# Turns of the first expert layer rounded by ScalarE's integer write, and q's second order of halves copied instead of transposed

## The chip, the cores and the metric

One NeuronCore of a Trainium2 chip runs the whole program. The metric is the device time of one execution in microseconds (us), as the median of several executions. Beside it stands one profiled execution with its trace. The engines are named as the profile names them: PE (TensorE, with PEld for its weight loads), DVE (VectorE), ACT (ScalarE), POOL (GpSimd) and SP (SyncE, whose queue "SPq" issues all DMAs here).

## What is computed

Attention over 4 batches and 8 heads (1152 keys of 64 elements, q averaged in pairs to 576 rows), and behind it two dense layers over the 2304 tokens. The first has `h*cos(h)` as its nonlinearity, the second `h*sigmoid(h)`.

```python
q_pool = q.reshape(B, H, S // 2, 2, D).mean(axis=3)
scores = scale * np.matmul(q_pool, k.transpose(0, 1, 3, 2))
attn = softmax(scores)                      # with 1e-09 in the denominator
x = heads_side_by_side(np.matmul(attn, v))  # 2304 x 512
h = x @ w_in;   x = (h * np.cos(h)) @ w_out         # 512 -> 2048 -> 512
h = x @ w_in2;  out = (h / (1 + np.exp(-h))) @ w_out2
```

## The kernel before

**Halves.** Every matmul input is kept as two fp16 numbers, a high half and the rest ("low" half), which takes two or three fp16 matmuls for one product.

**Attention.** Two heads make a pair; there are 16 pairs (4 per batch). A pair has 9 tiles of 128 query rows, 144 in all. For a tile, PE writes scores into two PSUM tiles `sp` (line 549), DVE scales them into `sc` and takes their minimum (line 568), ACT takes the exponential (line 576) and writes the high half `hl` (line 582), POOL writes the low half in three pieces (line 150, called from line 587), SP issues one DMA transpose of both halves, 18 blocks of 128x128 (line 589), and PE multiplies by v (lines 600, 604). Up to four tiles are in flight.

**Preparing a pair** (`pair_prep`, lines 473 to 532) runs during the tiles of the pair before: maxima on DVE (line 127), a scale, then the halves of q, k and v. For q the array `qn` holds the halves twice, once in the order high|low and once low|high, because keys come as high|low and both products are wanted: ACT writes the high half in two places (line 509), DVE the low half (line 510) and a second copy of it (line 513), and one DMA transpose of 18 blocks makes `qT` (line 515). `kn` is split by ACT and DVE (lines 466, 471) and transposed, 18 blocks (line 525).

**First layer.** It works on 9 blocks of 256 tokens. A unit is 12 matmuls: 16 units of the first product (`h`, line 685) and 16 of the second (`y`, line 740) in a block. From batch 1 on, two units are handed out for each attention tile; what remains comes behind attention, beside the preparation of the second layer's weights. Two units of the first product fill one PSUM tile; there are two of these. ACT copies it to `hk`, scaled so that 1 is a full turn (line 701). Four units make a group `hk` of 128x1024, 36 groups in all. Then `g_cos_begin` works out the distance to the nearest whole turn on DVE: line 713 adds 0.25 and a large number that rounds, line 714 subtracts the number and `hk`. ACT takes the sine (line 720), DVE multiplies (line 723) and writes the high half `gh` (line 728), POOL the low half `gl` (line 150). The array `tt` has two buffers; a block's result `y32` (line 749), on its way to DRAM, uses the same two.

**Second layer.** Behind that PE alternates between the second layer's two products.

**What sets the order.** Each engine runs its own list in order. The lists are made when the program is built, by a scheduler that works with priorities and its own time model. A change of one instruction can so move others.

Of the kernel before, what the change touches and what calls it, by code (L numbers as in the profile page):

```python
# [11 lines left out]
F32 = mybir.dt.float32  # L12
F16 = mybir.dt.float16
I32 = mybir.dt.int32
AF = mybir.ActivationFunctionType
ALU = mybir.AluOpType
# [2 lines left out]
DRAM = bass.MemoryType.DRAM  # L19

EXP_MASK = 0x7F800000
MAGIC = 12582912.0
TINY = 2.0**-50
W_MIN = float(np.array([0x38100000], np.uint32).view(np.float32)[0])
END = object()
P_CH, P_SC, P_EX, P_PV, P_MS, P_MU, P_W, P_PR, P_X = 0, 60, 0, -100, 200, 0, 0, 0, 0
PSH = 15.0
NB_N, NB_SC, NB_H, NB_T, NB_S = 2, 4, 4, 4, 5
LOW_HL, LOW_G, LOW_W = 3, 2, 2
X_LAG = 40  # L30
W1_BUFS, WT_BUFS = 3, 3
# [8 lines left out]
NB_HK, NB_TT, NB_G, SIN_N = 2, 2, 2, 2  # L40
# [9 lines left out]
def attention_moe_moe_kernel(ctx, tc, q, k, v, w_in1, w_out1, w_in2, w_out2, out):  # L50
# [3 lines left out]
    nc = tc.nc  # L54
    B, H, S, D = q.shape
# [4 lines left out]
    KC = S // 128  # L60
# [5 lines left out]
    const = ctx.enter_context(tc.tile_pool(name="const", bufs=1))  # L66
# [6 lines left out]
    mean = const.tile([128, 128], F32, name="mean")  # L73
    halfpi = const.tile([128, 1], F32, name="halfpi")
    floor3 = const.tile([128, 1], F32, name="floor3")

    def make_consts():
        nc.vector.memset(mean, 2.0**-7)
        nc.vector.memset(halfpi, math.pi / 2)
        nc.vector.memset(floor3, 2.0**-14 - 0.5)  # L80

    GW = 256

# [389 lines left out]
    def pair_prep(at, P):  # L473
        NQ = 2 * NT + 1
        qs = P.q[:, :, 0, :]
# [28 lines left out]
            split(vt[:, :, 0, 0:D], vt[:, :, 1, 0:D], P.v[i], s[:, 2:3], P.on_pool >= 2)  # L504


        qn = at.src.tile([128, 2, NQ, 2, D], F16, tag="kn", name="qn", bufs=NB_N)
        for e in range(2):
            nc.scalar.activation(out=qn[:, e, :, e, :], in_=qs, func=AF.Copy, scale=s[:, 0:1])
        nc.vector.scalar_tensor_tensor(  # L510
            out=qn[:, 0, :, 1, :], in0=qs, scalar=s[:, 0:1], in1=qn[:, 0, :, 0, :], op0=ALU.mult, op1=ALU.subtract
        )
        nc.vector.tensor_copy(qn[:, 1, :, 0, :], qn[:, 0, :, 1, :])
        qT = at.p.tile([128, 2, NQ, 128], F16, tag="qT", name="qT", bufs=2)
        nc.sync.dma_start_transpose(
            out=qT.rearrange("p e n k -> p (e n) k"), in_=qn.rearrange("p e n s d -> p (e n s d)")
        )
        P.qT = [qT[:, e] for e in range(2)]
        yield
        kn = at.src.tile([128, 2, KC, 2, D], F16, tag="kn", name="kn", bufs=NB_N)  # L520
        for i in range(2):
            split(kn[:, i, :, 0, :], kn[:, i, :, 1, :], P.k[i], s[:, 1:2], P.on_pool >= 1)
            yield
# [6 lines left out]
        for i in range(2):  # L530
            do_v(i)
            yield

    segs = [(o, min(512, S - o)) for o in range(0, S, 512)]

# [155 lines left out]
    def g1_evac(mp, w, blk, f, first):  # L691
        if f % 2 == 0:
            return
        g = f * w.npc // NF
        if first:
            if f % 4 == 1:
                blk.hk = mp.p.tile([128, 4, GW], F32, tag="hk", name="hk", bufs=NB_HK)
            o = blk.hk[:, (f % 4) - 1:(f % 4) + 1, :]
        else:
            o = blk.view(f - 1, 2)  # L700
        nc.scalar.activation(  # L701
            out=o, in_=blk.hp, func=AF.Copy if first else AF.Silu, scale=blk.c.a[:, g:g + 1]
        )

    def g_cos_begin(mp, blk):

        G = Block()
        G.hk, G.K = blk.hk, blk.c.k
        G.gh = mp.p.tile([128, 4, GW], F16, tag="gh", name="gh", bufs=NB_G)
        G.gl = mp.p.tile([128, 4, GW], F16, tag="gl", name="gl", bufs=NB_G)  # L710
        blk.g.append((G.gh, G.gl))
        G.t = t = mp.p.tile([128, 4, GW], F32, tag="tt", name="tt", bufs=NB_TT)
        nc.vector.tensor_scalar(out=t, in0=G.hk, scalar1=0.25, scalar2=MAGIC, op0=ALU.add, op1=ALU.add)
        nc.vector.scalar_tensor_tensor(out=t, in0=t, scalar=MAGIC, in1=G.hk, op0=ALU.subtract, op1=ALU.subtract)
        return G

    def g_cos_end(groups):
# [553 lines left out]
```

## Time and profile before

| | |
|---|---|
| median of 3 runs | 1358.67 us (1353.96 to 1359.51) |
| the profiled execution | 1361.32 us, span of the trace 1359.5 us |
| busy in the span | PE 1146.0 (84%), PEld 914.5 (67%), DVE 981.6 (72%), ACT 870.0 (64%), POOL 705.1 (52%) |
| DMA queue | 509,472 packets, 65.7% of 16 engines over the span |
| granted TensorE clock | 0.916 of full speed over the span |

The span has four stages, told apart by what PE does: attention alone (0 to about 240 us), attention with units of the first layer (240 to about 816), the rest of the first layer beside the weights of the second (816 to about 1059), and the second layer (1059 to the end). A busy share says how much of a stretch an engine worked; the waits say what ended the idle time before an instruction.

### The profile page before, as it was taken

What the parts mean: (1) busy time and instruction counts of PE and PEld (TensorE: products, weight loads), DVE (VectorE), ACT (ScalarE), POOL (GpSimd) and SP (SyncE); (2) the same over time, 40 slices, a digit from 0 to 9 for tenths busy, and PEclk for the clock granted to TensorE, in tenths of its full rate; (3) what the DMA queues carried; (4) which work ended last, traced back from release to release, by engine and by line L of the source; (5) the groups of instructions that cost most, each with busy time, mean ns of one, the idle gap of its engine ahead of it and who ended that gap; (6) DMA issues with size and microseconds to landing.
All of it is one profiled execution on the core that took longest, in us unless ns stands there. A gap on an engine that the chain in (4) does not pass through costs nothing. (4 is left out here: it accounts for less than half of the span.)

```text
span 1359.5 us, 26737 instructions
## 1 busy us (share of the span) xinstructions
PE 1146.0 (84%) x10668; PEld 914.5 (67%) x10668; DVE 981.6 (72%) x1927; ACT 870.0 (64%) x1061; POOL 705.1 (52%) x624
## 2 busy tenths in 40 slices
PE   1564565888988679998898999899999999999998
PEld 0333343666766456675676677788788888888887
DVE  6896978877877777795787795986757755444483
ACT  3896888778777777885788774634546633333352
POOL 1688686688668576875768673533667400000000
PEclk9677676989999888998999999999899999999999
DMA  9999999889799999998999975413344000000001
GB/s 270 210 229 219 224 242 208 152 159 175 139 191 186 195 201 202 191 162 161 164 181 190 197 174 100 128 60 75 82 97 106 32 30 27 9 16 17 17 32 32
DMA packets 509597, 186.29 MB, mean 137 GB/s; under 512 B 465952, under 2 KB 484384, under 8 KB 509472
## 3 DMA queue, kind: packets, MB, share of 16 engines
q1 hardware_dynamic: 509472, 184.59, 65.7%
q8 instruction: 83, 1.36, 0.4%
q14 instruction: 42, 0.34, 0.1%
HBM read 66.58 MB, written 9.44 MB: 56 GB/s over the span
## 5 line engine op out<-in xcount | busy, mean ns | idle before, releaser
L150 POOL TENSOR_TENSOR hl<-sc,hl 128x384 f16<-128x384 f32 x432 | 453.8, 1081 | 145.3 <-ACT hl L582 110.1
L568 DVE TENSOR_SCALAR_CACHE_REDUCE sc<-sp,psu 128x512 f32<-128x512 f32 (+1 forms) x288 | 229.7, 808 | 78.1 <-PE sp L549 66.9
L549 PE MATMUL sp<-kT,qT 128*128 128x512 f16 (+1 forms) x768 | 195.3, 373 | 83.5 <-DVE sc L568 58.7
L685 PEld LDWEIGHTS <-ih 128*128 128x128 f16 x2304 | 226.3, 100 | 45.7 <-issue 13.8
L600 PE MATMUL pv<-vt,hlT 128*128 128x130 f16 (+1 forms) x1440 | 194.6, 236 | 73.8 <-DMA hlT<-hl 68.2
L576 ACT ACTIVATE sc<-sc,nb 128x1152 f32<-128x1152 f32 x144 | 179.4, 1249 | 76.8 <-DVE nb L573 69.7
L600 PEld LDWEIGHTS <-hlT 128*128 128x128 f16 (+1 forms) x1440 | 144.6, 109 | 106.3 <-DMA hlT<-hl 80.9
L685 PE MATMUL h<-ys,ih 128*128 128x256 f16 x1152 | 195.6, 274 | 4.1 <-ACT gs L701 4.1
L685 PE MATMUL h<-xT,ih 128*128 128x256 f16 x1024 | 186.3, 277 | 5.1 <-ACT hk L701 2.1
L604 PE MATMUL pv<-vt,hlT 128*128 128x65 f16 (+1 forms) x1440 | 184.7, 206 | 0.0
L582 ACT ACTIVATE hl<-sc 128x1152 f16<-128x1152 f32 x144 | 165.2, 1154 | 26.2 <-DMA hlT<-hl 20.0
L549 PEld LDWEIGHTS <-qT 128*128 128x128 f16 x768 | 77.1, 109 | 150.9 <-issue 102.5
L740 PE MATMUL y<-gh,oh 128*128 128x256 f16 x576 | 162.8, 283 | 6.8 <-ACT y L749 6.8
L740 PE MATMUL y<-gl,oh 128*128 128x256 f16 x576 | 163.1, 283 | 1.9 <-POOL gl L150 1.9
L740 PE MATMUL y<-gh,ol 128*128 128x256 f16 x576 | 162.6, 282 | 0.0
L854 PEld LDWEIGHTS <-op 128*128 128x128 f16 x1512 | 147.9, 98 | 18.0 <-issue 0.6
L685 PE MATMUL h<-ys,il 128*128 128x256 f16 x576 | 157.7, 274 | 0.0
L604 PEld LDWEIGHTS <-hlT 128*128 128x128 f16 (+1 forms) x1440 | 141.2, 107 | 14.6 <-issue 7.1
L685 PE MATMUL h<-xT,il 128*128 128x256 f16 x512 | 141.8, 277 | 0.0
L150 POOL TENSOR_TENSOR gl<-tt,gh 128x512 f16<-128x512 f32 (+1 forms) x60 | 97.3, 1637 | 79.7 <-DVE gh L728 61.0
L740 PEld LDWEIGHTS <-oh 128*128 128x128 f16 x1152 | 115.4, 102 | 30.8 <-issue 10.3
L685 PEld LDWEIGHTS <-il 128*128 128x128 f16 x1152 | 114.2, 99 | 16.9 <-issue 0.4
(310 smaller groups left out, 1967.6 us busy)
## 6 DMA issues: line engine op xcount, KB each, us to landing
wst<-in_moe_w_in_dram SPq DMA_DIRECT2D x16, 1024.0 KB, 6.1
stk<-in_k_dram SPq DMA_DIRECT2D x32, 288.0 KB, 4.2
stv<-in_v_dram SPq DMA_DIRECT2D x32, 288.0 KB, 4.4
stq<-in_q_dram SPq DMA_DIRECT2D x32, 256.0 KB, 3.1
wst<-in_moe_w_out_dram SPq DMA_DIRECT2D x8, 1024.0 KB, 6.4
wst<-in_moe_w_out_dram SPq DMA_DIRECT2D x16, 512.0 KB, 6.0
ydr<-y SPq DMA_DIRECT2D x9, 512.0 KB, 3.3
y32b<-ydr SPq DMA_DIRECT2D x9, 512.0 KB, 3.3
```

What stands on the lines that cost most here:

```text
L150: last = nc.gpsimd.tensor_tensor(out=lo[:, o:o + w], in0=x[:, o:o + w], in1=hi[:, o:o + w], op=ALU.subtract)
L549: nc.tensor.matmul(sp[:, o - a:o - a + n], P.qT[e][:, t, :], kT[:, o:o + n], start=(e == 0), stop=(e == 1))
L568: nc.vector.tensor_scalar(out=T.sc[:, a:z], in0=sp, scalar1=T.P.su, scalar2=None, op0=ALU.mult, op1=ALU.min, accum_out=mx[:, x:x + 1],)
L576: nc.scalar.activation(out=T.sc, in_=T.sc, func=AF.Exp, scale=-1.0, bias=nb)
L582: nc.scalar.activation(out=hi, in_=T.sc, func=AF.Copy)
L600: nc.tensor.matmul(G.pv[r, T.gi], T.hlT[:, 0, c, r], P.vt[i][:, c], start=(c == 0), stop=(c == KC - 1), skip_group_check=True,)
L604: nc.tensor.matmul(G.pv[r, T.gi, 0], T.hlT[:, 1, c, r], P.vt[i][:, c, 0], start=False, stop=(c == KC - 1), skip_group_check=True,)
L685: nc.tensor.matmul(hp, wt[:, c, f * 128:(f + 1) * 128], xt(c), start=(i == 0), stop=(i == 3 * NC - 1), skip_group_check=True,)
L740: nc.tensor.matmul(blk.y[:, oc, :], wt[:, f, oc * 128:(oc + 1) * 128], gt[:, f % 4, :], start=(f == 0 and e == 0 and oc % 2 == 0), stop=(f ...
L854: nc.tensor.matmul(bank, t[:, e, c, :], wt[:, c, :], start=start, stop=True, skip_group_check=True)
```

## The change

Two edits.

1. *Turns.* The array `tt` is now taken together with `hk`, at the first of a group's two evictions. ACT reads each PSUM tile a second time and writes `hk + 0.25` into `tt` as a 32-bit integer, which rounds to a whole turn. On DVE the two instructions of lines 713 and 714 become one, integer minus `hk`.
2. *q.* `qn` holds the halves once. One ACT instruction writes the high half, one DVE instruction the low half, and the DMA transpose has 9 blocks where it had 18. The other order is made from the result: two ACT copies of 64 partitions x 1152 elements swap the upper and the lower 64 partitions. They stand at the end of the pair's preparation, with a step of their own. `qn` and `kn` have one buffer each, where they shared two.

```diff
-        qn = at.src.tile([128, 2, NQ, 2, D], F16, tag="kn", name="qn", bufs=NB_N)
-        for e in range(2):
-            nc.scalar.activation(out=qn[:, e, :, e, :], in_=qs, func=AF.Copy, scale=s[:, 0:1])
-        nc.vector.scalar_tensor_tensor(
-            out=qn[:, 0, :, 1, :], in0=qs, scalar=s[:, 0:1], in1=qn[:, 0, :, 0, :], op0=ALU.mult, op1=ALU.subtract
-        )
-        nc.vector.tensor_copy(qn[:, 1, :, 0, :], qn[:, 0, :, 1, :])
+        qn = at.src.tile([128, NQ, 2, D], F16, tag="qn", name="qn", bufs=1)
+        split(qn[:, :, 0, :], qn[:, :, 1, :], qs, s[:, 0:1], False)
         qT = at.p.tile([128, 2, NQ, 128], F16, tag="qT", name="qT", bufs=2)
-        nc.sync.dma_start_transpose(
-            out=qT.rearrange("p e n k -> p (e n) k"), in_=qn.rearrange("p e n s d -> p (e n s d)")
-        )
+        nc.sync.dma_start_transpose(out=qT[:, 0], in_=qn.rearrange("p n s d -> p (n s d)"))
...
+        for x, y in ((slice(0, 64), slice(64, 128)), (slice(64, 128), slice(0, 64))):
+            nc.scalar.activation(out=qT[x, 1], in_=qT[y, 0], func=AF.Copy)
+        yield
...
         nc.scalar.activation(
             out=o, in_=blk.hp, func=AF.Copy if first else AF.Silu, scale=blk.c.a[:, g:g + 1]
         )
+        if first:
+            nc.scalar.activation(
+                out=blk.tt.bitcast(I32)[:, (f % 4) - 1:(f % 4) + 1, :], in_=blk.hp, func=AF.Identity,
+                scale=blk.c.a[:, g:g + 1], bias=quarter,
+            )
...
-        nc.vector.tensor_scalar(out=t, in0=G.hk, scalar1=0.25, scalar2=MAGIC, op0=ALU.add, op1=ALU.add)
-        nc.vector.scalar_tensor_tensor(out=t, in0=t, scalar=MAGIC, in1=G.hk, op0=ALU.subtract, op1=ALU.subtract)
+        nc.vector.tensor_tensor(out=t, in0=t.bitcast(I32), in1=G.hk, op=ALU.subtract)
```

The numbers of instructions change so: ACT 72 more for the turns, 32 more for the copies, 16 fewer for q; DVE 36 and 16 fewer; POOL, PE and SP as many as before.

At the end of a block of the first layer, ACT's list before reads as follows. Here `hk_4221` is the last group of the block that is being computed, `h_4139` and `h_4292` are its two PSUM tiles, and `y32_4112` is the result of the block before it.

```order
L701 ACTIVATE hk_4221<-h_4139,ca_2647 128x512 [waits PE_49]
L623 ACTIVATE x32_2855<-pvs_4044,den_4041 128x64 [waits DVE_49]
L623 ACTIVATE x32_2856<-pvs_4044,den_4041 128x64 x2
L749 ACTIVATE y32_4112<-y_2903,cy_2371 128x256 [waits Pool_49]
L749 ACTIVATE y32_4112<-y_2903,cy_2371 128x256 x3
L576 ACT_TABLE_LOAD
L576 ACTIVATE sc_4231<-sc_4231,nb_4235 128x1152 [waits DVE_49]
L576 ACTIVATE sc_4313<-sc_4313,nb_4317 128x1152 [waits DVE_49]
L582 ACTIVATE hl_4238<-sc_4231 128x1152 [waits DMAHW2_49,Activation_49]
L582 ACTIVATE hl_4320<-sc_4313 128x1152 [waits DMAHW4_49,Activation_49]
L576 ACTIVATE sc_4396<-sc_4396,nb_4400 128x1152 [waits DVE_49]
L701 ACTIVATE hk_4221<-h_4292,ca_2647 128x512 [waits PE_49]
```

And this is the same place in the changed kernel, where the group is `hk_4228` with its `tt_4229`.

```order
L751 ACTIVATE y32_4119<-y_2907,cy_2373 128x256 [waits Pool_49]
L751 ACTIVATE y32_4119<-y_2907,cy_2373 128x256 x3
L699 ACTIVATE hk_4228<-h_4146,ca_2650 128x512 [waits PE_49]
L620 ACTIVATE x32_2853<-pvs_4052,den_4049 128x64 [waits DVE_49]
L573 ACTIVATE sc_4240<-sc_4240,nb_4244 128x1152 [waits DVE_49]
L573 ACTIVATE sc_4322<-sc_4322,nb_4326 128x1152 [waits DVE_49]
L699 ACTIVATE hk_4228<-h_4301,ca_2650 128x512 [waits PE_49]
L579 ACTIVATE hl_4247<-sc_4240 128x1152 [waits DMAHW2_49,Activation_49]
L579 ACTIVATE hl_4329<-sc_4322 128x1152 [waits DMAHW4_49,Activation_49]
L703 ACTIVATE tt_4229<-h_4146,quarter_75,ca_2650 128x512 [waits DMAHW2_49]
L703 ACTIVATE tt_4229<-h_4301,quarter_75,ca_2650 128x512
L573 ACTIVATE sc_4405<-sc_4405,nb_4409 128x1152 [waits DVE_49,Pool_49]
```

The two new writes stand together behind `y32` and wait for a DMA, the transfer of `y32` that frees their buffer; until then both PSUM tiles stay taken. In ACT's list 8 of the 36 groups have such a wait for a DMA at the first new write, and 20 one for POOL (the low half of an earlier group).

The preparation of a pair, here the 14th, reads on ACT before:

```order
L509 ACTIVATE qn_7899<-stq_7454,ps__7868 128x9x64 [waits DMAHW1_49,DMAHW0_49,DVE_49]
L509 ACTIVATE qn_7899<-stq_7454,ps__7868 128x9x64
L466 ACTIVATE kn_7932<-stk_7455,ps__7868 128x9x64
L582 ACTIVATE hl_7962<-sc_7955 128x1152 [waits DMAHW7_49,Activation_49,Pool_49]
L466 ACTIVATE kn_7932<-stk_7456,ps__7868 128x9x64 [waits DMAHW0_49]
L466 ACTIVATE vt_108<-stv_7457,ps__7868 128x9x64 [waits DMAHW1_49,PE_49]
L466 ACTIVATE vt_111<-stv_7458,ps__7868 128x9x64 [waits DMAHW2_49,PE_49]
```

And in the changed kernel:

```order
L467 ACTIVATE qn_7917<-stq_7510,ps__7886 128x9x64 [waits DVE_49]
L467 ACTIVATE kn_7948<-stk_7511,ps__7886 128x9x64
L467 ACTIVATE kn_7948<-stk_7512,ps__7886 128x9x64
L467 ACTIVATE vt_109<-stv_7513,ps__7886 128x9x64 [waits PE_49]
L467 ACTIVATE vt_112<-stv_7514,ps__7886 128x9x64 [waits DMAHW7_49,PE_49]
L620 ACTIVATE x32_5326<-pvs_7943,den_7940 128x64 [waits DVE_49]
L579 ACTIVATE hl_7978<-sc_7971 128x1152 [waits DMAHW7_49,Activation_49,Pool_49]
L573 ACTIVATE sc_8030<-sc_8030,nb_8034 128x1152 [waits DVE_49]
L528 ACTIVATE qT_7920<-qT_7920 64x1152 [waits DMAHW1_49]
L528 ACTIVATE qT_7920<-qT_7920 64x1152
```

One write of `qn` is gone, and the two copies, which wait for the transpose, have come in behind v's halves and in front of the next tiles' exponentials.

## Rows read from the trace of the kernel before

**Rows 1.** Windows by stage: busy time of each engine, granted clock, DMA share, GB/s.
```profile
core 0: us, PE busy (x) PEld busy (x) DVE busy (x) ACT busy (x) POOL busy (x), PEclk, DMA share, GB/s
0.00:240.00 240.00, 127.38 (x993) 79.62 (x994) 194.70 (x454) 180.55 (x202) 160.38 (x156) 0.72 1.02 228
240.00:816.00 576.00, 498.82 (x4993) 376.83 (x4991) 448.76 (x977) 444.24 (x529) 407.39 (x375) 0.94 0.94 178
816.00:1059.00 243.00, 225.03 (x1990) 194.72 (x1991) 175.28 (x262) 121.98 (x161) 128.67 (x87) 0.95 0.40 93
1059.00:1360.00 301.00, 294.76 (x2696) 263.38 (x2695) 162.85 (x236) 123.26 (x173) 8.62 (x9) 1.00 0.06 22
```

**Rows 2.** Waits, 30 to 240 us: who waited for whom, us, times, longest.
```profile
PE pv L600 <- DMA hlT<-hl: 46.7, 22, 5.0
PE sp L549 <- DVE sc L568: 21.1, 19, 4.0
```

**Rows 3.** Waits, 240 to 816 us.
```profile
POOL hl L150 <- ACT hl L582: 80.1, 32, 7.0
...
DVE sc L568 <- PE sp L549: 55.4, 38, 6.2
ACT sc L576 <- DVE nb L573: 52.5, 25, 8.6
PE sp L549 <- DVE sc L568: 36.6, 29, 5.3
...
PE pv L600 <- DMA hlT<-hl: 19.1, 11, 3.4
...
PE sp L549 <- DMA kT<-kn: 9.3, 2, 5.1
```

**Rows 4.** Timeline of SP's queue: start, us, what, how many.
```profile
575.14 19.24 SPq L589 DMA_TRANSPOSE hlT<-hl  x4
594.82 2.84 SPq L515 DMA_TRANSPOSE qT<-qn  x1
597.82 2.74 SPq L589 DMA_TRANSPOSE hlT<-hl  x1
```

**Rows 5.** Lines 515, 1115 and 671: SP's time, ns min/median/max, of transposes of 18, 8, 16 blocks.
```profile
L515 SPq DMA_TRANSPOSE qT<-qn x16: 2697/2839/3931, 17.1 to 747.9; - x16
L1115 SPq DMA_TRANSPOSE xrT<-xnr x2: 1231/1232/1232, 867.6 to 874.7; - x2
L671 SPq DMA_TRANSPOSE xT<-xn x8: 1600/1831/3089, 249.3 to 842.3; - x8
```

**Rows 6.** Groups, 240 to 816 us: count | busy us, mean ns | idle before, releasers.
```profile
L576 ACT ACTIVATE sc<-sc,nb 128x1152 f32<-128x1152 f32 x105 | 131.1, 1250 | 58.1 <-DVE nb L573 52.5 <-DVE den L616 2.7 <-DVE xs L116 1.7
L582 ACT ACTIVATE hl<-sc 128x1152 f16<-128x1152 f32 x106 | 121.6, 1155 | 13.6 <-DMA hlT<-hl 7.4 <-DMA xT<-xn 5.1
L714 DVE SCALAR_TENSOR_TENSOR tt<-tt,hk 128x1024 f32<-128x1024 f32 x23 | 33.2, 1445 | 0.1
L701 ACT ACTIVATE hk<-h,ca 128x512 f32<-128x512 f32 x47 | 31.5, 675 | 13.4 <-PE h L685 13.4
L713 DVE TENSOR_SCALAR tt<-hk 128x1024 f32<-128x1024 f32 x23 | 21.4, 928 | 5.9 <-ACT hk L701 5.4 <-ACT hl L582 0.4
L513 DVE COPY qn<-qn 128x576 f16<-128x576 f16 x11 | 5.7, 519 | 0.1
L509 ACT ACTIVATE qn<-stq,ps__8521 128x576 f16<-128x576 f32 x2 | 1.4, 763 | 0.0
```

**Rows 7.** Groups, 816 to 1059 us.
```profile
L701 ACT ACTIVATE hk<-h,ca 128x512 f32<-128x512 f32 x25 | 17.0, 681 | 12.6 <-PE h L685 12.5
L713 DVE TENSOR_SCALAR tt<-hk 128x1024 f32<-128x1024 f32 x13 | 10.7, 823 | 11.2 <-ACT hk L701 10.4 <-DMA ydr<-y 0.8
L779 DVE TENSOR_TENSOR gs<-gs 128x1024 f32<-128x1024 f32 x2 | 3.0, 1476 | 0.0
```

**Rows 8.** Timeline of ACT and SP at a block's end: start, us, what.
```profile
612.91 1.55 ACT L749 ACTIVATE y<-y,cy 128x256 f32<-128x256 f32 x4
614.33 0.70 ACT L701 ACTIVATE hk<-h,ca 128x512 f32<-128x512 f32 x1
...
616.10 0.52 SPq L752 DMA_DIRECT2D ydr<-y  x1
```

**Rows 9.** Chain that ended last, where weights give way to the second layer; DMA issues.
```profile
1050.21 2.65 POOL wst L360 x2
...
1059.64 2.78 PE h L685 x24
...
ydr<-y SPq DMA_DIRECT2D x9, 512.0 KB, 3.3
```

More of the change, by code (lines that the diff above doesn't have):

```diff
@@ L21 @@
 EXP_MASK = 0x7F800000
-MAGIC = 12582912.0
 TINY = 2.0**-50
@@ L27 @@
 PSH = 15.0
-NB_N, NB_SC, NB_H, NB_T, NB_S = 2, 4, 4, 4, 5
+NB_SC, NB_H, NB_T, NB_S = 4, 4, 4, 5
 LOW_HL, LOW_G, LOW_W = 3, 2, 2
@@ L75, in attention_moe_moe_kernel @@
     floor3 = const.tile([128, 1], F32, name="floor3")
+    quarter = const.tile([128, 1], F32, name="quarter")
     def make_consts():
@@ L80, in make_consts @@
         nc.vector.memset(floor3, 2.0**-14 - 0.5)
+        nc.vector.memset(quarter, 0.25)
     GW = 256
@@ L504, in do_v @@
             split(vt[:, :, 0, 0:D], vt[:, :, 1, 0:D], P.v[i], s[:, 2:3], P.on_pool >= 2)
-        qn = at.src.tile([128, 2, NQ, 2, D], F16, tag="kn", name="qn", bufs=NB_N)
-        for e in range(2):
-            nc.scalar.activation(out=qn[:, e, :, e, :], in_=qs, func=AF.Copy, scale=s[:, 0:1])
-        nc.vector.scalar_tensor_tensor(
-            out=qn[:, 0, :, 1, :], in0=qs, scalar=s[:, 0:1], in1=qn[:, 0, :, 0, :], op0=ALU.mult, op1=ALU.subtract
-        )
-        nc.vector.tensor_copy(qn[:, 1, :, 0, :], qn[:, 0, :, 1, :])
+        qn = at.src.tile([128, NQ, 2, D], F16, tag="qn", name="qn", bufs=1)
+        split(qn[:, :, 0, :], qn[:, :, 1, :], qs, s[:, 0:1], False)
         qT = at.p.tile([128, 2, NQ, 128], F16, tag="qT", name="qT", bufs=2)
-        nc.sync.dma_start_transpose(
-            out=qT.rearrange("p e n k -> p (e n) k"), in_=qn.rearrange("p e n s d -> p (e n s d)")
-        )
+        nc.sync.dma_start_transpose(out=qT[:, 0], in_=qn.rearrange("p n s d -> p (n s d)"))
         P.qT = [qT[:, e] for e in range(2)]
         yield
-        kn = at.src.tile([128, 2, KC, 2, D], F16, tag="kn", name="kn", bufs=NB_N)
+        kn = at.src.tile([128, 2, KC, 2, D], F16, tag="kn", name="kn", bufs=1)
         for i in range(2):
@@ L697, in g1_evac @@
                 blk.hk = mp.p.tile([128, 4, GW], F32, tag="hk", name="hk", bufs=NB_HK)
+                blk.tt = mp.p.tile([128, 4, GW], F32, tag="tt", name="tt", bufs=NB_TT)
             o = blk.hk[:, (f % 4) - 1:(f % 4) + 1, :]
@@ L711, in g_cos_begin @@
         blk.g.append((G.gh, G.gl))
-        G.t = t = mp.p.tile([128, 4, GW], F32, tag="tt", name="tt", bufs=NB_TT)
-        nc.vector.tensor_scalar(out=t, in0=G.hk, scalar1=0.25, scalar2=MAGIC, op0=ALU.add, op1=ALU.add)
-        nc.vector.scalar_tensor_tensor(out=t, in0=t, scalar=MAGIC, in1=G.hk, op0=ALU.subtract, op1=ALU.subtract)
+        G.t = t = blk.tt
+        nc.vector.tensor_tensor(out=t, in0=t.bitcast(I32), in1=G.hk, op=ALU.subtract)
         return G
```

## The prediction

> **What bounds the kernel now.** First the windows by stage [rows 1]. In the second layer (from 1059 us) TensorE is busy 294.8 of 301 us at full clock: nothing that the change touches works there, so it only moves that stage as a whole. From 816 to 1059 TensorE is busy 225.0 of 243 us and idle for 18. The two attention stages are different: no compute engine is full. From 0 to 240 us DVE is busy for 81% and ACT for 75%, but the DMA engines show a share of 1.02. From 240 to 816 us PE stands at 87%, DVE at 78%, ACT at 77%, POOL at 71%, and DMA at 0.94. So the fullest resource of attention is the DMA path, and the next question is whether somebody waits for it.
>
> The waits answer that. Early, the largest single entry of PE is the transposed weights of attention, 46.7 us in 22 waits, more than twice what it waits for DVE's scores, 21.1 [rows 2]. Later PE waits 36.6 us for DVE, and 19.1 + 9.3 = 28.4 us for transposes, of 576 - 498.8 = 77.2 us idle in all [rows 1, 3]. SP's queue shows the same from the other side: four transposes of `hl` stand without a gap for 19.24 us, with one of q and the next of `hl` right behind [rows 4]. A transposition that is half as long lets everything behind it in this queue go earlier. ACT is waited for through POOL: 80.1 us in 32 waits for the high half `hl` [rows 3], of 576 - 407.4 = 168.6 us in which POOL is idle. ACT itself mostly waits for DVE's minimum, 52.5 us.
>
> So I read attention as a pipeline in which DMA is the bound at the beginning and shares the end with the loop between PE's scores and DVE later on, while ACT still has 132 us of room in the second stage (576 - 444.2).
>
> **Term A, the shorter transposes before 240 us.** A transposition of 18 blocks takes SP 2.84 us; one of 8 blocks takes 1.23, one of 16 blocks 1.83 [rows 5]. Nine blocks lie between these: 1.23 to 1.83, and I take half of 2.84, 1.42, which is nearest to the row of 8 blocks. One shorter transposition so frees 1.0 to 1.6 us, taken as 1.4. Five of the 16 are issued before 240 us. With DMA at 1.02 nearly all of 5 x 1.4 = 7.0 us should arrive; ACT's additional work for them (below, 1.55 us each) has cover in its 25% of idle time. I take 6 us, with 0 and 8 as ends.
>
> **Term B, the same after 240 us.** Eleven transposes give 11 x 1.4 = 15.4 us on SP and DMA. Of PE's idle time 28.4 of 77.2 us, 37%, ends with a transposition, so I take 37% of it, 5.7 us. Ends: 0 (hidden) and 15.4.
>
> **Term C, what DVE loses, 240 to 816 us.** Line 713 goes: 21.4 us in 23 instructions. Line 513 goes: 5.7 us in 11 [rows 6]. Line 714 becomes an instruction with two tensors and one subtraction. The trace has none with an integer operand; the nearest is line 779, two tensors of the same size, 1476 ns against the 1445 of line 714 [rows 6, 7], so the price stays as it is. In all 27.1 us less. PE's waits for DVE are 36.6 of 77.2 us, 47%. But DVE also waits 55.4 us for PE's scores [rows 3], so that an earlier DVE often only waits longer. I take half of the 47%: 27.1 x 0.47 / 2 = 6.4 us. Ends: 0 and 12.8.
>
> **Term D, what ACT gets, 240 to 816 us.** The new write reads the same PSUM tile of 512 elements as `hk`, 675 ns [rows 6]. It has a bias from memory beside the scale from memory. What that costs is read from two instructions of one size: the exponential with a bias from memory takes 1250 ns, the copy without 1155, a difference of 95 ns [rows 6]. So 0.675 to 0.77 us, and I take 0.77: 47 x 0.77 = 36.2 us. The Trainium skill ("ScalarE: Activation LUTs", What ACT_TABLE_LOAD costs) says that each operand of one value a partition adds about 93 ns; the two rows agree with that. A copy of 64 partitions x 1152 elements is not in the trace. The nearest row is `hl`, 128 x 1152, 1155 ns; half of it would be the lower end if partitions counted, and I keep 1155, since in ACT's rows the time goes with the elements of a partition: 512 take 675, 576 take 763, 1152 take 1155. Two copies less one write of `qn` (763 ns) are 2 x 1.155 - 0.76 = 1.55 us a pair, 11 x 1.55 = 17.0 us. Together 53.2 us, and ACT goes from 77% to 86% in this stage. How much of that comes through? PE hardly waits for ACT itself; it goes through `hl`, POOL and the transposition. POOL's waits for `hl` are 80.1 of 168.6 us, 47.5%, so at most 25 us if each such wait became longer in proportion; nothing if ACT's 132 idle us take it. I take a third of the upper end, 8.4 us, because ACT's own waits are mostly for DVE, which gets earlier in the same stage. Without that cover it costs the 25.
>
> The copies stand at the end of the preparation, where they wait for a DMA. Queued behind them on ACT are the exponentials of the next tiles, and the scores of the next pair wait for the copies. The copies come some six instructions after `qn`, though, and the transposition is issued 1.4 us sooner, so I put nothing down for that. The new `tt` writes wait in 20 places for POOL and in 8 for the transfer of a block's result. One such place in the trace: `y` is done at 614.46, the second `hk` of the half group at 615.03, the transfer is issued at 616.10 and takes 3.3 us, so until about 619.4 [rows 8, 9]. Written right behind `hk`, the first new write would hold ACT for some 4.4 us, 35 us in 8 places. In the changed order two exponentials and two `hl` (4.8 us) stand in between, and cover it. In their shadow the two PSUM tiles stay taken, and PE goes on with scores and with units of the second product.
>
> **Term E, 816 to 1059 us.** DVE loses 10.7 us, ACT gets 25 x 0.77 = 19 us, while it is busy for 122 of 243 [rows 1, 7]. The chain to 1059 us goes through POOL's preparation of weights into PE's `h` [rows 9], and PE has 18 idle us. I take a gain of 2 us. Ends: 10 us of gain (all of DVE's), and 8 of loss (two of the waits for POOL or the transfer at full length).
>
> **Sum.** 6 + 5.7 + 6.4 - 8.4 + 2 = 11.7 us less. The profiled execution took 1361.3 us, so 1349.6; it lies 2.6 us above the median of the runs, on whose scale the sum gives 1358.7 - 11.7 = 1347.0 us. This is my forecast, with a range of its own from 1338 to 1353: the lists of all engines are rewritten, and a pair whose q and k come late can cost PE some 5 us more or less (one wait for `kT` lasted 5.1 us [rows 3]).
>
> **The rivals.**
>
> *ACT becomes the bound (slower).* It speaks for this that ACT would be the fullest of DVE, ACT and POOL at 86%, that it runs in order, and that 28 new waits stand in its list; against it that only 80.1 us of anybody's idle time in this stage ends with its `hl`, and that it is idle for 132 us. It decides from the point at which ACT's gaps, which DVE opens, no longer fall where the new writes stand. Then D costs 25 and E loses 5: -6 - 5.7 - 6.4 + 25 + 5 = 12 us more, 1371 us. The Trainium skill ("ScalarE: Activation LUTs", Rules for kernel authors) would have simple adds and multiplies on VectorE and not on ScalarE; rows 6 bear the price out, 1.54 us of ACT for 0.93 us of DVE, but the rule says nothing of which engine ends last, and by it alone the time would be this rival's.
>
> *Nothing left over (same).* PE's loop with DVE sets attention after 240 us, transposes are hidden there, and ACT's additional work eats what the first stage gives: -6 + 5 - 1 = 2 us less, 1357 us. For it: 55.4 and 36.6 us of waits between PE and DVE in both directions.
>
> *All of the DMA time arrives (much faster).* The queue is the bound up to 816 us, and ACT's work stays under it: -7 - 15.4 - 6.4 - 2 = 31 us less, 1328 us. For it the share of 0.94; against it that PE waits more for DVE than for transposes in that stage.
>
> *The change doesn't do what it says.* If the copies cost ACT what the transposition saved on the way to the first score of a pair, B and A vanish and D stays: about 1354 to 1359, inside the second rival.
>
> **How the numbers follow.** Forecast 0.45, ACT bound 0.17, nothing left over 0.27, all arrives 0.11. About 0.5% (6.8 us, 1351.9 to 1365.5) is what a measurement of this kernel tells from no change. Faster: the forecast less its upper edge, and all arrives, 0.53. Same: nothing left over and that edge, 0.30. Slower: 0.17. The range from 1328 to 1370 leaves out the lower half of the last case and over half of the first rival, together under 0.2.
>
> **What would show it.** A and B: SP's time for q's transposes near 1.4 us, and fewer us of PE waiting for `hlT`, before 240 us above all; the stage that ended at 240 should end at about 234. C: line 713 gone, PE's wait for DVE's `sc` smaller than 36.6 us. D: the new writes at 0.77 us and the copies at 1.16 us; ACT near 86%; POOL's wait for `hl` grown by less than 25 us. It would be wrong if POOL's wait for `hl` and PE's for `hlT` grew together (ACT is the bound), or if the `tt` writes were preceded by long idle time of ACT that ends with POOL's `gl` or with the transfer.

## The result

The changed kernel takes 1322.47 us (median of four runs, 1320.70 to 1323.76), the kernel before in the same session 1356.96 us (1353.96 to 1359.51). The ratio is 0.9746, with a 95% interval from 0.9718 to 0.9773: 34.5 us faster. The forecast was 1347.0 us, in a range from 1328 to 1370. So the sign was right, and the time lies below the range, below even the case in which all of the DMA time arrives.

The windows by stage of the changed kernel come first, to be held against [rows 1]; the columns are the same.

```profile
core 0: us, PE busy (x) PEld busy (x) DVE busy (x) ACT busy (x) POOL busy (x), PEclk, DMA share, GB/s
0.00:240.00 240.00, 131.53 (x1021) 83.24 (x1021) 196.84 (x460) 191.59 (x210) 160.87 (x159) 0.72 1.01 223
240.00:816.00 576.00, 514.82 (x5237) 397.18 (x5238) 444.44 (x972) 498.58 (x601) 418.22 (x381) 0.95 0.92 177
816.00:1059.00 243.00, 226.25 (x2054) 200.92 (x2053) 175.79 (x243) 147.09 (x195) 129.52 (x84) 0.99 0.34 82
1059.00:1360.00 301.00, 257.80 (x2362) 230.72 (x2359) 136.23 (x202) 101.22 (x145) 0.00 (x0) 1.00 0.06 20
```

The first stage holds hardly more of PE's work than before (1021 matmuls against 993, of 10,668). From 240 to 816 us there are 5237 matmuls against 4993: this is where the kernel runs ahead. ACT is busy for 498.58 of 576 us, 86.6%, as forecast, and is now next to PE.

Where the time went is told most simply by two lines of the program: the last transposition of `hl` (the end of attention) and the first matmul of the second layer. The next lines are of the kernel before: duration in ns (min/median/max), then the start of the first and of the last.

```profile
L589 SPq DMA_TRANSPOSE hlT<-hl x144: 2459/2923/6950, 36.7 to 824.7; - x144
L854 PE MATMUL oy<-ops,op x864: 269/273/283, 1070.4 to 1352.0; 128*128 128x256 f16 x173
```

And the same two of the changed kernel:

```profile
L586 SPq DMA_TRANSPOSE hlT<-hl x144: 2322/2852/5883, 33.3 to 793.8; - x144
L856 PE MATMUL oy<-ops,op x864: 269/273/273, 1032.8 to 1314.4; 128*128 128x256 f16 x173
```

Attention ends 824.7 - 793.8 = 30.9 us earlier. From there to the second layer it is 239.0 us where it was 245.7, 6.7 us less. The second layer is as long as before (281.6 us from its first to its last such matmul). Counted in transposes of `hl`, the 36th starts at 234.9 us (237.7 before) and the 37th at 239.7 (241.4). So the first 240 us gave 2 to 3 us, the stage behind it some 28, the rest of the first layer 6.7. The 28 us don't come evenly: from the start of the 96th transposition to that of the 116th it takes 99.8 us where it took 118.1, so 18.3 us lie in these 20 tiles.

The spans of the two profiled executions, 1359.5 and 1321.9 us, are 37.6 us apart. PE's idle time makes 22.0 of them. The other 15.6 are PE's busy time, which fell from 1146.0 to 1130.4 us for the same 10,668 matmuls, while the granted clock over the span went from 0.916 to 0.928. One place at which the two hang together is shown in the first section of the experiments.

Next the pieces of the change, each by its own line. They are the lengths to be held against [rows 5] and [rows 6].

```profile
L511 SPq DMA_TRANSPOSE qT<-qn x16: 1243/1314/3762, 14.9 to 712.6; - x16
...
L528 ACT ACTIVATE qT<-qT x32: 1161/1162/1164, 21.0 to 718.9; 64x1152 f16<-64x1152 f16 x32
...
L703 ACT ACTIVATE tt<-h,quarter,ca x72: 754/769/791, 258.2 to 933.6; 128x512 int32<-128x512 f32 x72
  POOL gl L151: 5.9, 5
  DMA ydr<-y: 1.5, 2
...
L716 DVE TENSOR_TENSOR tt<-tt,hk x36: 1208/1248/2150, 262.3 to 938.1; 128x1024 f32<-128x1024 int32 x36
```

Each size is close to what was put down: 1314 ns for the shorter transposition (1.42 us), 1162 ns for a copy (1155), 769 ns for a `tt` write (770). Under line 703 stands what ACT sat idle for before these writes: 5.9 us for POOL and 1.5 us for the transfer of a block's result, in the whole kernel. The feared places are covered.

Last the waits, of the stretch from 30 to 240 us first (who waited for whom, us, times, longest), for [rows 2].

```profile
PE sp L546 <- DVE sc L565: 39.4, 22, 7.2
POOL hl L151 <- ACT hl L579: 35.5, 14, 5.8
...
PE pv L597 <- DMA hlT<-hl: 27.3, 12, 5.7
DVE pm L128 <- DMA stk<-in_k_dram: 16.4, 4, 5.7
```

PE's wait for `hlT` fell from 46.7 to 27.3 us, as the prediction wanted, but its wait for DVE's scores rose from 21.1 to 39.4, and DVE itself waits 16.4 us for the loads of k. One wait stands where the other stood, and hardly anything was left over.

From 240 to 816 us, for [rows 3]:

```profile
POOL hl L151 <- ACT hl L579: 57.1, 25, 8.6
DVE sc L565 <- PE sp L546: 41.9, 29, 8.5
...
PE sp L546 <- DVE sc L565: 32.2, 23, 5.1
...
PE pv L597 <- DMA hlT<-hl: 15.9, 11, 2.4
...
ACT sc L573 <- DVE nb L570: 12.7, 14, 2.1
```

POOL waits less for ACT than before (57.1 us against 80.1), although ACT has 54 us more to do; ACT's own wait for DVE's minimum went from 52.5 to 12.7 us. ACT used its gaps. But the waits named in the sum moved by only a few us each (32.2 against 36.6, 15.9 against 19.1), and some 28 us are gone from the stage. That is not the picture of a sum that came out larger; so the first question was what the lists' new order does alone.

### The profile page after: what moved, and what is told of

Read it like the earlier page. It is cut to its first block, busy times and chain, and to the rows that moved or that the text cites. A ratio compares the mean times of both kernels' runs of the same rounds, so it can differ in the third digit from the quotient of the medians.

```text
span 1321.9 us, 26728 instructions
## 1 busy us (share of the span) xinstructions
PE 1130.4 (86%) x10668; PEld 912.1 (69%) x10668; DVE 953.3 (72%) x1876; ACT 938.5 (71%) x1147; POOL 708.6 (54%) x624
## 5 line engine op out<-in xcount | busy, mean ns | idle before, releaser
L682 PEld LDWEIGHTS <-ih 128*128 128x128 f16 x2304 | 225.5, 99 | 48.4 <-issue 18.1
L597 PEld LDWEIGHTS <-hlT 128*128 128x128 f16 (+1 forms) x1440 | 146.7, 110 | 78.5 <-DMA hlT<-hl 50.6
L742 PE MATMUL y<-gh,oh 128*128 128x256 f16 x576 | 158.6, 275 | 4.8 <-ACT y L751 4.8
L742 PE MATMUL y<-gl,oh 128*128 128x256 f16 x576 | 158.5, 275 | 2.1 <-POOL gl L151 2.1
L742 PE MATMUL y<-gh,ol 128*128 128x256 f16 x576 | 158.6, 275 | 0.0
L601 PEld LDWEIGHTS <-hlT 128*128 128x128 f16 (+1 forms) x1440 | 142.5, 108 | 16.1 <-issue 8.1
L151 POOL TENSOR_TENSOR gl<-tt,gh 128x512 f16<-128x512 f32 (+1 forms) x60 | 102.8, 1728 | 60.8 <-DVE gh L730 58.6
L742 PEld LDWEIGHTS <-oh 128*128 128x128 f16 x1152 | 112.6, 99 | 24.2 <-issue 7.0
```

The source lines that it names most:

```text
L151: last = nc.gpsimd.tensor_tensor(out=lo[:, o:o + w], in0=x[:, o:o + w], in1=hi[:, o:o + w], op=ALU.subtract)
L597: nc.tensor.matmul(G.pv[r, T.gi], T.hlT[:, 0, c, r], P.vt[i][:, c], start=(c == 0), stop=(c == KC - 1), skip_group_check=True,)
L601: nc.tensor.matmul(G.pv[r, T.gi, 0], T.hlT[:, 1, c, r], P.vt[i][:, c, 0], start=False, stop=(c == KC - 1), skip_group_check=True,)
L682: nc.tensor.matmul(hp, wt[:, c, f * 128:(f + 1) * 128], xt(c), start=(i == 0), stop=(i == 3 * NC - 1), skip_group_check=True,)
L742: nc.tensor.matmul(blk.y[:, oc, :], wt[:, f, oc * 128:(oc + 1) * 128], gt[:, f % 4, :], start=(f == 0 and e == 0 and oc % 2 == 0), stop=(f ...
```

## Experiments

All times are medians beside the kernel before, which was 1356 to 1359 us in every session; ratios have 95% intervals.

### Each edit alone, an empty step, and both without the step

The change has two edits, and the second brings a `yield` of its own, a further step in a pair's preparation, by which the scheduler hands out the work at other moments. Four kernels take this apart.

First edit alone (turns), on the kernel before:

```diff
+            nc.scalar.activation(
+                out=blk.tt.bitcast(I32)[:, (f % 4) - 1:(f % 4) + 1, :], in_=blk.hp, func=AF.Identity,
+                scale=blk.c.a[:, g:g + 1], bias=quarter,
+            )
...
+        nc.vector.tensor_tensor(out=t, in0=t.bitcast(I32), in1=G.hk, op=ALU.subtract)
```

> The kernel before with the first edit alone: whole turns written as integers by ScalarE, one DVE instruction in place of two; q as before (18-block transposes, no copies). Theory 'DMA' (the 34.5 us come from the shorter transposes of q): 0 to 6 us less than before, 1351 to 1357. Theory 'DVE' (they come from the 27 us that DVE loses in the stage with units, and from the shorter way to the low half gl): 20 to 30 us less, 1327 to 1337. Theory 'order' (a luckier order of the lists): either, with no relation to the parts.

Measured: 1345.36 us, 0.9888 (0.9852 to 0.9924).

Second edit alone (q), with its step:

```diff
+        nc.sync.dma_start_transpose(out=qT[:, 0], in_=qn.rearrange("p n s d -> p (n s d)"))
...
+        for x, y in ((slice(0, 64), slice(64, 128)), (slice(64, 128), slice(0, 64))):
+            nc.scalar.activation(out=qT[x, 1], in_=qT[y, 0], func=AF.Copy)
+        yield
```

> The kernel before with the second edit alone: 9-block transposes of q, the other order copied by ScalarE, one more step in a pair's preparation; turns as before on DVE. Theory 'DMA': 25 to 34 us less than before, 1323 to 1332, and PE's waits for hlT and kT after 240 us down from 28 us. Theory 'DVE': 0 to 8 us less. If both parts give their share, about 15 us each.

Measured: 1340.25 us, 0.9847 (0.9812 to 0.9883).

The step alone, in the kernel before; no instruction is added or taken away:

```diff
         for i in range(2):
             do_v(i)
             yield
+        yield
```

> The kernel before with nothing but one empty step at the end of a pair's preparation, as the second edit has it: the next pair's loads are taken up half a tile later, and the lists come out in another order. No work is added or removed. Theories 'DMA' and 'DVE': within 5 us of before. Theory 'order': 10 us or more off before, to either side; that is also the size of what a new order alone can do here.

Measured: 1338.88 us, 0.9844 (0.9804 to 0.9884). An empty step is worth as much as either edit. Here too PE's busy time for the same matmuls is shorter, 1130.5 us.

Both edits without the additional step (the copies stand in the step of the last v):

```diff
         for i in range(2):
             do_v(i)
-            yield
+            if not i:
+                yield
```

> The changed kernel with the copies of q moved into the last step of v's halves, so that the preparation has as many steps as before. The work is that of the changed kernel. Theories 'DMA' and 'DVE': within 5 us of the changed kernel, 1317 to 1327. Theory 'order': 10 us or more above it.

Measured: 1339.34 us, 0.9835 (0.9791 to 0.9878). Without the boundary between two steps 17 us of the gain are gone.

What does an empty step change? In the lists of the two kernels every engine's instructions are the same up to about the 60th of the 144 tiles, and in another order behind that. In the traces most of the difference lies in one stretch. Six tiles (the 106th to the 111th) take 44 us in the kernel before, from 616.7 to 660.9 us by the starts of their transposes, and 30 us with the step (613.5 to 643.2). The windows of these stretches, of the kernel before:

```profile
618.00:662.00 44.00, 38.72 (x374) 28.25 (x372) 32.13 (x69) 25.47 (x30) 27.81 (x25) 0.88 0.76 149
```

and of the kernel with the empty step (same columns as above):

```profile
612.00:642.00 30.00, 29.27 (x315) 22.04 (x313) 25.09 (x62) 23.06 (x31) 21.75 (x20) 1.00 0.95 181
```

Before, ACT is busy for 58% there and DMA for 76%; with the step 77% and 95%. In the timeline of DVE in the kernel before (start, us, what, idle time before it and who ended it) stands how it begins:

```profile
614.69 0.21 DVE L573 TENSOR_SCALAR nb<-mx 128x1 f32<-128x1 f32 x1
...
619.75 0.75 DVE L127 TENSOR_REDUCE pm<-stq 128x1 f32<-128x576 f32 x1 [4.86 <-POOL stq L476]
620.54 0.15 DVE L487 COPY pm<-pm 128x1 f32<-128x1 f32 x1
624.09 0.75 DVE L127 TENSOR_REDUCE pm<-stk 128x1 f32<-128x576 f32 x1 [3.40 <-DMA stk<-in_k_dram]
```

The maxima of the next pair's q and k stand in DVE's list ahead of data that has not come: 4.86 and 3.40 us in which DVE, which runs in order, does nothing for the tiles in flight. The waits of the whole stretch from 605 to 662 us show who starves:

```profile
POOL gl L150 <- DVE gh L728: 15.9, 2, 9.0
ACT sc L576 <- DVE nb L573: 13.6, 3, 8.6
...
DVE pm L127 <- POOL stq L476: 4.9, 1, 4.9
DVE pm L127 <- DMA stk<-in_k_dram: 3.4, 1, 3.4
```

With the empty step DVE's waits for these data are 1.4 us (k) and 1.3 us (v) in the corresponding stretch.

The stretch has a second cost. PE finds no scores to go on with: it stands still for 4.48 us, from 622.04 to 626.52, and that wait ends with DVE's `sc`:

```profile
626.52 1.01 PE L549 MATMUL sp<-kT,qT 128*128 128x512 f16 x2 [4.48 <-DVE sc L568]
```

In the windows of these moments (same columns) the granted clock, the last number but two, falls to 0.50, the lower of its two levels (1.2 and 2.4 GHz):

```profile
620.00:626.00 6.00, 2.04 (x27) 1.51 (x25) 2.37 (x5) 1.76 (x3) 6.00 (x8) 0.98 0.99 243
626.00:632.00 6.00, 5.48 (x19) 2.08 (x18) 5.28 (x12) 1.61 (x2) 1.54 (x2) 0.50 0.59 126
632.00:638.00 6.00, 6.00 (x48) 4.00 (x48) 2.94 (x6) 3.13 (x3) 3.62 (x4) 0.67 0.33 25
```

Behind the pause a matmul of 256 columns (128 x 256) takes 0.39 us where it took 0.27 in front of it, and the clock is full again from about 636 us on. PE so works for 9.5 us at half clock; by an estimate from these windows that costs some 5 of the 14 us. In the kernel with the empty step the clock stays at 1.00 over the whole stretch. That the two in-order waits of DVE start the long stretch is read from the trace; that they and the pause account for all of the 14 us was not tried. The long stretch isn't the kernel's of before alone: over all kernels of this document these six tiles take 41 to 45 us in five, and 28 to 36 us in the others.

### Four paces for each content

If an empty step moves the time by 20 us, one order for each kernel says little of an edit. So each of the four contents was run at four paces: no additional step; one at the end of the preparation; two at the end; and one in front, behind the addition that averages q's pairs of rows:

```diff
         m = small.tile([128, 5], F32, name="pm", tag="pm")
+        yield
         for i in range(2):
             absmax(m[:, 1 + i:2 + i], P.k[i], AX.XY)
```

The kernel before, with two steps and with one in front:

> The kernel before with two empty steps at the end of a pair's preparation; no work changes. Theory 'parts add up' with a step that helps because the next pair's loads are taken up later: about the same as one step or better, 1325 to 1342. Theory 'any order': anywhere in 1335 to 1360.

> The kernel before with one empty step at the start of a pair's preparation instead of its end; no work changes. The loads of the next pair move by the same half tile as with the step at the end, and the maxima move too. Theory 'a later load helps': 1335 to 1345, as with the step at the end. Theory 'any order': anywhere in 1335 to 1360.

The turns, with one step, two, and one in front:

> The kernel before with the first edit (turns) and one empty step at the end of a pair's preparation; q as before. So far against before: turns alone -14 us, the empty step alone -20 us, both edits with the step -34.5. Theory 'parts add up' (turns give about 14, the step gives about 20 by itself, q's shorter transposes next to nothing): 1322 to 1328. Theory 'any order' (each order of the lists draws its own time, within some 20 us): anything from 1325 to 1350, with no sum.

> Turns alone (first edit), with two empty steps at the end of a pair's preparation. The same four paces (no step, one or two at the end, one in front) are run for each content: before 1358, 1339, 1343, 1363 us, mean 1351. Theory 'the turns themselves give about 12 us, on top of a scatter of some 20 us by the order': 1322 to 1342. Theory 'order only': 1335 to 1363.

> Turns alone, with one empty step in front of a pair's preparation. Theory 'the turns give about 12 us': 1340 to 1355, under the 1363 of the kernel before at this pace. Theory 'order only': no relation to 1363, anywhere in 1330 to 1363.

q, without a step, with two, and with one in front:

> The kernel before with the second edit (q's 9-block transposes and the copies), the copies in the last step of v's halves, so that no step is added; turns as before. Theory 'parts add up': q gives next to nothing without the step, 1350 to 1360. Theory 'any order': from 1335 on. If the shorter transposes do count: 1335 to 1345.

> q's edit alone (9-block transposes and copies; turns as before), with two empty steps at the end of a pair's preparation. Theory 'q's edit gives about 10 us': 1328 to 1342. Theory 'order only': 1335 to 1363.

> q's edit alone, with one empty step in front of a pair's preparation. Theory 'q's edit gives about 10 us': 1340 to 1355. Theory 'order only': anywhere in 1335 to 1363.

Both, with two steps and with one in front:

> Both edits, with two empty steps at the end of a pair's preparation. Means over the four paces so far: before 1351 us, turns alone 1333, q alone 1335. Theory 'each edit gives its 17 us whatever the other does': mean 1317, so 1308 to 1328 here. Theory 'the second edit finds the room of the first used (ACT is then the fullest)': mean 1328 to 1333, so 1320 to 1342 here.

> Both edits, with one empty step in front of a pair's preparation. Theory 'each edit gives its 17 us': 1308 to 1330. Theory 'the room is used': 1322 to 1342.

With one step at the end q's copies have that step to themselves; at the other three paces they stand in the step of the last v. All sixteen medians, in us (the intervals of the ratios are 0.005 to 0.009 wide, 6 to 12 us; the kernel before is put down with 1358):

| content | no step | one at the end | two at the end | one in front | mean |
|---|---|---|---|---|---|
| before | 1358 | 1338.9 | 1343.5 | 1363.1 | 1350.9 |
| turns | 1345.4 | 1326.8 | 1328.4 | 1331.7 | 1333.1 |
| q | 1334.7 | 1340.3 | 1330.0 | 1333.8 | 1334.7 |
| both | 1339.3 | 1322.5 | 1329.5 | 1329.5 | 1330.2 |

Three things follow. The order alone moves the kernel before over 24 us, from 1338.9 to 1363.1. At the same pace an edit alone is faster than no edit in seven of eight cases (q with one step, +1.4 us, is the exception), and both together are faster in all four, by 18.7, 16.4, 14.0 and 33.6 us, 20.7 in the mean. And the edits don't add in the mean: the turns alone give 17.8 us, q alone 16.2, both 20.7 and not 34. This third point is the weakest. At the changed kernel's own pace, one step at the end, the turns give 12.1 us, q nothing (1.4 more), and both give 16.4, more than the sum; at the other three both give less than it, by 15 to 27 us.

By this table the 35.5 us between 1358 and 1322.5 are 20.7 for the content, 7.1 because the kernel before stands above the mean of its four orders, and 7.7 because the changed one is the best of its four. At one and the same pace it is simpler: the empty step alone takes 1358 to 1338.9 us, the two edits take that to 1322.5, 16.4 us. With four orders each the means are rough. The differences at the four paces scatter so that the standard error of a mean is 4.6 us for the turns, 6.7 for q and 4.4 for both: the gains of the turns and of both are clear of nought, q's is not quite.

### Is q's gain DMA time?

To the q edit a second transposition of 9 blocks was added, into an array that nobody reads, so that SP and DMA have as much to do as before. It was run at the paces with no step and with one in front.

```diff
         nc.sync.dma_start_transpose(out=qT[:, 0], in_=qn.rearrange("p n s d -> p (n s d)"))
+        q2 = at.src.tile([128, NQ, 128], F16, tag="q2", name="q2", bufs=1)
+        nc.sync.dma_start_transpose(out=q2, in_=qn.rearrange("p n s d -> p (n s d)"))
```

> q's edit alone without a step (1334.7 us), but SP issues a second transposition of the same 9 blocks into an array that nobody reads, so that the DMA engines move as much as before. ACT's copies and DVE's saved copy are as with q's edit. Theory 'q's 17 us come from the shorter transposes': 1345 to 1362. Theory 'from DVE's saved copy or the order': 1328 to 1342.

> q's edit alone with one empty step in front of the preparation (1333.8 us), and the second transposition that nobody reads, so that the DMA engines move as much as before. Without a step this took all of the gain back, 1335 to 1355. Theory 'q's gain is DMA time': 1348 to 1368 (the kernel before takes 1363 at this pace). Theory 'the first of these was one unlucky order': 1328 to 1345.

Measured: 1355.34 us, 0.9986 (0.9969 to 1.0003), against 1334.7 without it; and 1341.74 us, 0.9892 (0.9865 to 0.9920), against 1333.8. The two transposes of the first of these kernels:

```profile
L510 SPq DMA_TRANSPOSE qT<-qn x16: 1242/1296/1619, 14.3 to 744.6; - x16
...
L512 SPq DMA_TRANSPOSE q<-qn x16: 1348/1394/4500, 16.0 to 749.5; - x16
```

Sixteen times 1.39 us are 22.3 us of SP's queue, and they cost 20.6 and 7.9 us, 14.3 in the mean, of the 23.3 and 29.3 that q gives at these paces. The stage from 240 to 816 us of the kernel with the second transposition:

```profile
240.00:816.00 576.00, 496.54 (x4961) 377.58 (x4961) 441.67 (x954) 461.38 (x540) 408.61 (x374) 0.94 0.93 177
```

and of the kernel without it:

```profile
240.00:816.00 576.00, 514.33 (x5172) 390.01 (x5169) 463.91 (x985) 466.58 (x549) 421.81 (x383) 0.96 0.92 177
```

4961 matmuls against 5172, 211 fewer, and with that about as many as in the kernel before (4993 [rows 1]). In both pairs PE's busy time over the whole kernel stays as it is (1143.2 us with the second transposition and 1143.0 without, 1131.1 and 1130.4), so what is lost is PE's idle time. Both losses speak for the queue's time as a part of q's gain, at the one pace nearly all of it. How large a part is not settled: an additional instruction also changes the lists, an empty step alone moves the time by up to 24 us, and the two losses don't lie in the same tiles. At the first pace 13.7 us of it lie from the 96th to the 116th tile, where at the second the kernel with more to transpose is 13.0 us *faster*.

The Trainium skill ("Perfetto Trace Analysis", What "DMA-bound" means) counts a kernel as bound by DMA too where the issuing engine's track is solid with DMA work; SP's row of four transposes without a gap, 19.24 us [rows 4], and the sign of these two runs agree with it. Over the whole stage from 240 to 816 us SP's issues cover some 460 of the 576 us in the kernel before, 80%.

### Is the turns' gain DVE's time?

To the turns a multiplication of `hk` by 1 was added on DVE, in place and ahead of the subtraction:

```diff
         G.t = t = blk.tt
+        nc.vector.tensor_scalar(out=G.hk, in0=G.hk, scalar1=1.0, scalar2=0.0, op0=ALU.mult, op1=ALU.add)
         nc.vector.tensor_tensor(out=t, in0=t.bitcast(I32), in1=G.hk, op=ALU.subtract)
```

> The turns' edit alone without a step (1345.4 us), but DVE multiplies hk by 1 in place ahead of the subtraction, so that it has as many and as long instructions as before and the chain of the turns is as long; ACT's 72 additional writes stay. Theory 'the turns' 18 us come from what DVE loses': back to the mean of before or above it, 1348 to 1370, for ACT's work is added and nothing given. Theory 'order': 1330 to 1350.

> The turns alone with one empty step in front (1331.7 us), and DVE's multiplication of hk by 1 in place, so that DVE has as much work as before. Without a step this stayed at 1335, though DVE had its time back. Theory 'the turns' gain is DVE time': 1345 to 1368. Theory 'it is not; the wait for a tt buffer, which went from DVE's list to ACT's, or the order': 1325 to 1342.

The groups of the first, 240 to 816 us (count | busy us, mean ns | idle before):

```profile
L722 DVE TENSOR_TENSOR tt<-tt,hk 128x1024 f32<-128x1024 int32 x24 | 35.9, 1496 | 1.9 <-ACT tt L708 1.7 <-DVE hk L721 0.2
L721 DVE TENSOR_SCALAR hk<-hk 128x1024 f32<-128x1024 f32 x24 | 20.2, 842 | 7.7 <-ACT hk L704 7.7
```

1496 + 842 = 2338 ns for a group, against 928 + 1445 = 2373 in [rows 6]: DVE has its load back. Measured: 1334.63 us, 0.9832 (0.9808 to 0.9857), 10.7 us *less* than the turns without it (1345.4); and with the step in front 1343.27 us, 0.9901 (0.9866 to 0.9936), 11.6 us more (1331.7). The mean is nearly nought. Two orders don't show that the turns are faster because DVE has less to do, and don't exclude some 10 us of it.

One part of the turns' gain has a place. Behind attention, from the last transposition of `hl` to the second layer, the kernel with the turns alone takes 1053.0 - 814.3 = 238.7 us, by these lines:

```profile
L591 SPq DMA_TRANSPOSE hlT<-hl x144: 2372/2896/9702, 35.3 to 814.3; - x144
...
L861 PE MATMUL oy<-ops,op x864: 269/273/273, 1053.0 to 1334.5; 128*128 128x256 f16 x173
```

At all four paces it is 239 to 241 us, where the kernel before and its three other orders take 243 to 247 and q alone 244. With DVE's load put back it is 242.4 and 242.6 us. So some 5 us of the turns' gain lie in the rest of the first layer, and both orders lose 3 to 4 of them again with DVE's load. But with both edits two orders take 239.0 us and two 244.5 and 246.0: the order alone moves this stage by as much, so that these 3 to 4 us are DVE's time is likely and not shown. Inside attention the two orders contradict each other, and there the cause stays open. A wait for a `tt` buffer that left DVE's list is hardly it: before, DVE sat idle ahead of line 713 for 5.9 us from 240 to 816 us, 5.4 of them for ACT's `hk` [rows 6], and behind it 0.8 us for the transfer [rows 7].

## Why the prediction was wrong

The forecast was 11.7 us less, and 34.5 were measured. Three steps failed. The order of the lists was allowed 5 us, where it alone moves the kernel before by 24. Of term A's 7.0 us nearly all were to arrive, and 2 to 3 did. And the sum counts only waits: PE's busy time, for which it puts nothing, fell by 15.6 us for the same matmuls. Besides, terms B and E were too small, the loss of term D can't be seen, and how much of term C came is open.

*What bounds the kernel.* It read DMA as the bound at the beginning and as one of two later. The runs look the other way round: at the beginning a wait for DVE and for loads stood right behind the wait for `hlT`, and later the queue seems to have decided more than PE's waits showed.

*Term A, 6 us before 240 us.* Failed: 2 to 3 us arrived, and the empty step alone, without a shorter transposition, gives as much there (the 36th transposition starts at 234.7 us). The step that failed is "with DMA at 1.02 nearly all should arrive". The share of 1.02 is still 1.01; PE's wait for `hlT` did shrink, by 19.4 us, but its wait for DVE's scores grew by 18.3, from 21.1 to 39.4 us.

*Term B, 5.7 us of 15.4.* Probably mis-sized. q alone gives 16.2 us in the mean of four paces, though nothing at the pace of the changed kernel, and putting the queue's time back takes 20.6 and 7.9 us away. The step to blame is the one that gives the queue a share of the gain as large as the share of PE's idle time that ends with a transposition, 37%. SP's queue runs in order, and everything behind a shorter transposition moves forward: the loads and the `kT` with which a pair starts too. That this is how it reaches PE is argued; that the queue's time counts is what the sign of two runs says, not their size.

*Term C, 6.4 us.* Its size is neither confirmed nor refuted. Line 713 is gone, and the new subtraction costs as much as the old (1468 ns in line 716 below, 1445 before), as it assumed. The turns give 17.8 us in the mean, some 12 of them inside attention; that these are DVE's time was not shown.

*Term D, a loss of 8.4 us.* The path that it goes by, POOL's wait for `hl`, didn't lengthen: it fell from 80.1 to 57.1 us, and in the kernel before the order alone already moves it between 63 and 80. Every duration was right, ACT's 86% too, and the cover of the `tt` writes (7.4 us of idle time in 72 writes). With either edit alone no loss is to be seen in the mean. With both, the second edit adds 3 to 4.5 us in the mean instead of 16 to 18. ACT's idle time before the exponentials would fit a shared room, 20.8 us where it was 58.1 [rows 6]. The groups of the changed kernel, 240 to 816 us:

```profile
L716 DVE TENSOR_TENSOR tt<-tt,hk 128x1024 f32<-128x1024 int32 x24 | 35.2, 1468 | 9.7 <-POOL hl L151 5.2 <-ACT tt L703 4.3
...
L573 ACT ACTIVATE sc<-sc,nb 128x1152 f32<-128x1152 f32 x105 | 131.0, 1250 | 20.8 <-DVE nb L570 12.7 <-DVE den L613 3.0 <-DVE xs L117 1.7
```

That the two edits share anything is not clear of the scatter, and that it would be ACT's room is argued from this line, not shown by a run.

*Term E, 2 us.* Right in sign and mis-sized: 6.7 us, inside its ends. It is the turns' part (238.7 us with them alone). PE's idle time in this stage, which the term was measured by, fell by only 1.4 us, from 18.1 to 16.7; the other 5.3 us are PE's busy time, at a granted clock of 0.95 before and 0.99 with the change. The windows from the last transposition of `hl` to the second layer, of the kernel before:

```profile
824.70:1070.40 245.70, 227.59 (x1997) 197.76 (x1994) 173.00 (x264) 122.35 (x160) 128.80 (x88) 0.95 0.37 89
```

and of the changed kernel:

```profile
793.80:1032.80 239.00, 222.31 (x2064) 197.99 (x2061) 170.16 (x258) 139.16 (x187) 134.06 (x88) 0.99 0.38 92
```

*The order.* The largest error was one line: "the lists of all engines are rewritten, and a pair whose q and k come late can cost PE some 5 us more or less". The mechanism is the right one (DVE's maxima in front of q and k that are late), and the size was 24 us between the slowest and the fastest order of one and the same work. Half of it to either side of each case, 12 us, would have taken the lower end from 1328 to 1316 us. It was sized by one wait of 5.1 us, and not by a whole stretch in which the pipeline has run empty and fills again, though the trace of before has one that lasts 44 us. Where the order is worth 19 us by an empty step, and the changed kernel is the best of its four orders, a part of the 34.5 us is luck: at one and the same pace the edits give 16.4.

*PE's busy time.* The prediction names the clock for the second layer alone, and its sum puts nothing down for it. Of the 37.6 us between the two spans 15.6 are busy time for the same matmuls, and the empty step alone brings 15.5 (1146.0 to 1130.5 us). At 626 us of the kernel before the rows show how an idle PE comes to cost twice: 4.48 us of standing still, and half the clock for the 9.5 us behind it. That all of the 15.6 us come about in this way is not shown.

*The rivals.* ACT as the bound did not come. The Trainium skill ("ScalarE: Activation LUTs", Rules for kernel authors) would leave adds on VectorE; the runs differ from that here, since the kernel with the add moved to ScalarE was faster at each of four paces, by 12 to 31 us, at a higher price for the instruction. *Nothing left over* comes near for the first 240 us only. *All of the DMA time arrives* is the nearest for q after 240 us, as far as two runs tell. That the change does what it says is shown by the lengths.

## What to carry to other kernels

Where a scheduler orders the lists, run the old kernel with an empty step, and the parts of a change at several paces, before an edit gets the credit; here an edit's place in the order was worth as much as the edit. Time taken from an in-order queue that is nearly full can be worth more than the waits that bear its name, because all that stands behind it comes earlier. Two edits that lean on the same idle time need not add. And beside the idle time of PE its busy time for the same matmuls is to be compared before and after: here two fifths of the difference between the two profiled executions stood there.

## What the runs showed of the hardware

ACT's copy of 64 partitions x 1152 elements takes 1162 ns, as long as a write of 128 x 1152 from 32-bit numbers (1155 [rows 6]): half the partitions save nothing, and reading one half of the partitions while writing the other costs nothing that shows. ACT's write as a 32-bit integer, with its bias from memory, takes 769 ns for 512 elements where the plain write takes 675. And a transposition of 9 blocks takes SP 1.31 us, 1.39 for the second one in the kernel that makes two, where one of 18 blocks took 2.84 in the kernel before [rows 5]. Last, PE: in the kernel before it stood still for 4.48 us at 622 us, and the 9.5 us of work behind that ran at a granted clock of 0.50, a matmul of 256 columns in 0.39 us where it had taken 0.27.
